# An attention and feed-forward kernel: both halves of a block's scores in one run, an older block's values behind them in the same banks

## The chip, the cores and the metric

The kernel runs on one core of one Trainium2 chip. The metric is the device time of one execution in microseconds (us); the runs of one kernel are compared by their median. Durations inside an execution come from one profiled execution, on a scale that starts at its first instruction. TensorE is called PE, VectorE DVE, ScalarE ACT, GpSimd POOL and SyncE SP, as the profile does.

## What is computed

```python
# _attn_ref: q, k, v of (8, 8, 576, 64)
scores = scale * np.matmul(q, k.transpose(0, 1, 3, 2))
mask = (rel >= 0) & (rel < window)                 # window = 128
scores = np.where(mask, scores + bias[None], -1000000000.0)   # bias: -slope of the head * |rel|
scores = scores - np.max(scores, axis=-1, keepdims=True)
attn = np.exp(scores)
attn = attn / (np.sum(attn, axis=-1, keepdims=True) + 1e-09)
return np.matmul(attn, v)
# _moe_ref: on x of (8, 576, 512), the heads side by side
mu = np.mean(x, axis=-1, keepdims=True)
var = np.mean((x - mu) ** 2, axis=-1, keepdims=True)
xn = (x - mu) / np.sqrt(var + 1e-06) * g_ln
ch = np.maximum(xn @ w_ch1, 0.0) @ w_ch2           # 512 -> 2048 -> 512
return x + ch
```

A query sees itself and the 127 keys before it.

## The kernel before

**Tiling.** Batches go in four pairs. A block is 128 queries of one batch with all 8 heads; a pair has 9 of them (`NSLOT`), the two batches in turn, and the ninth (`blk == T`) joins the last 64 queries of both. There are 36 blocks, numbered n. A block's attention is: scores of keys against queries on PE (`attend`, L495, 64x64 quarters of the array), exp on ACT (L504), the product with the table of distances on DVE (`masks`, L516), values on PE (`values_at_once`, L579: 16 matmuls, 8 for a batch's first block with its single key tile, 24 for the ninth), division by the row sum on DVE (L587, L588), centring on DVE (`centre`, L616, L620) and a transposing DMA of the result from SP (L630). `square` (L664) sums its squares on ACT.

**Scores.** An ordinary block has two key tiles, and its scores come in two halves of four heads (`attends`): each half is 16 matmuls into one `ps_sc` tile of two banks, 1024 columns in all, and one exp over all of them. `seen` gives, for a key tile, the queries that it has to be computed for: of the two halves of queries one is often left out, since the table multiplies its weights by zero. Matmuls are then 128 or 64 columns wide. The exp reads the whole tile, so columns that were left out hold older scores. A batch's first two blocks have one key tile and one score tile with all heads ("own"); the ninth block has two halves against the last two full key tiles and one more tile for its own keys ("tail", `tail_attend`). Columns of the busiest quarter of the array, for one run of 16: 384 for an ordinary half, 512 with all queries, 512 for "own", 256 for the ninth block's halves and its tail.

**Banks.** PSUM holds four banks in turn for the linear layers (`ps_mm`) and two tiles `ps_sc[0]` and `ps_sc[1]` for attention. From block 8 on, values go to `ps_sc[0]` and all scores to `ps_sc[1]`.

**Linear layers.** Blocks are gathered into groups, `GROUPS = [2] * 4 + [4] * 7`; groups 4 to 10 have four blocks, 512 columns. `mlp1(g)` makes 16 units, one for each 128 hidden channels: four matmuls (L832) into a `ps_mm` bank, then relu on ACT (L848), for units 6 and 13 on DVE (L840). `mlp2_seven(g)` makes the second layer by Strassen's seven products: 28 units of four matmuls of 256 columns (L1062), four units for each product. Products share three banks x, t and y: product 0 (units 0 to 3) starts x, and DVE drains x into the output (L1083, two instructions); product 1 (units 4 to 7) uses t; product 2 (units 8 to 11) adds onto x, on the sums of hidden blocks; product 4 (units 16 to 19) adds onto x again after a further drain. The sums of hidden blocks are DVE's (`sum_hidden`, L882), placed in `mlp1` by `SUMS_AT` behind units 5, 8, 11, 14 and 15; those of 11 need the relu of unit 10. `mlp2_last` and `mlp1_last` serve group 10.

**Order.** All engines' queues are in the order in which the code issues (`manual_schedule`). `weave_at(units, *places)` runs a linear layer unit by unit and, behind unit u, first the sums of `SUMS_AT` and then as many attention steps as u stands in `places`. Up to n = 35 each block n >= 8 has four steps: (1) loads, the masks that are still open, values of n, centring of n, the first score tile of block n + 2 with its exp; (2) the second score tile with its exp; (3) masks of the first, `square`, and `turn_natural`, which has SP transpose queries of block n + 5 and keys of n + 6 by DMA; (4) masks of the second. The places of a group's stage are

```python
    TWICE = [4, 6, 8, 9, 11, 13, 15, 15], [3, 7, 11, 15, 19, 23, 27, 27]
```

the first list for `mlp1`, the second for `mlp2_seven`: two blocks in each. In group 4 the steps of n = 12 to 16 fall, then four blocks in each group, n = 33 to 35 in group 9.

Of the kernel before, what the change touches and what calls it, by code (L numbers as in the profile page):

```python
# [13 lines left out]
AF = mybir.ActivationFunctionType  # L14
# [8 lines left out]
T = 8  # L23
# [5 lines left out]
AHEAD = 7  # L29
# [13 lines left out]


V_FIRST = 20


SUMS_AT = {
# [44 lines left out]
def kernel(  # L93
# [10 lines left out]
    nc = tc.nc  # L104
# [330 lines left out]
            dst = t[:, b] if t is q else t[:, b].rearrange("p h (c r) -> p r h c", r=2)  # L435
            copy(out=dst, in_=ps[b][:, 0 if t is q else 1])  # L436

    weights_of, unmasked, scored = {}, {}, []

    def in_halves(t):  # L440
        return t if len(t.shape) == 3 else t.rearrange("p (r c) -> p r c", r=2)

    def seen(p, blk, o, t):


        both, every = slice(0, 2), slice(0, HALF)
        first, second = slice(0, HALF // 2), slice(HALF // 2, HALF)
        if p == 0 and blk < SEEN:
            return [(0, both, every), (1, both, every)]
        if blk == T:  # L450
            batches = [slice(0, 1), slice(1, 2)]
            return [(c, batches[c if o == T else t], every) for c in range(2)]
        if o == blk:
            return [(0, both, every), (1, both, second)]
        return [(1, both, every), (0, both, first)]
# [10 lines left out]
                skip_group_check=True,  # L466
            )

    def attend(p, blk, keys, mask, tag, hps, sc=None):

        heads = slice(2 * hps[0], 2 * hps[-1] + 2)
        nk = len(keys)
        if hps[0] == 0:
            pr = probs_pool.tile([P, H, nk, P], FP16, tag=tag, name=tag)
            for t, o in enumerate(keys):
                weights_of.setdefault((p, blk), []).append((pr, t, o))  # L480
        else:
            pr = weights_of[p, blk][-1][0]
        banks = ps_sc[len(scored) % 2 if sc is None else sc]
        scored.append((p, blk))
        ps = banks.rearrange("p j (n t q) -> p j n t q", n=len(hps), t=nk)
        added = p == 0 and blk < ADDED
        qt, b = turned["q", p, blk // 2], blk % 2
        for n, hp in enumerate(hps):
            for t, o in enumerate(keys):
                kt = turned["k", p, o // 2][:, o % 2]  # L490
                for c, r, queries in seen(p, blk, o, t):
                    cols = slice(c * HALF, (c + 1) * HALF)
                    for j in range(2):
                        rows = slice(j * HALF, (j + 1) * HALF)
                        nc.tensor.matmul(  # L495
                            in_halves(ps[cols, j, n, t, :])[:, r, queries],
                            kt[rows, hp, cols],
                            in_halves(qt[rows, b, hp])[:, r, queries],
                            start=not added,
                            stop=True,  # L500
                            skip_group_check=added,
                        )
        dst = pr[:, heads].rearrange("p h t q -> p h (t q)")
        nc.scalar.activation(  # L504
            out=dst.rearrange("p (n j) q -> p j n q", j=2),
            in_=ps.rearrange("p j n t q -> p j n (t q)"),
            func=AF.Exp,
            scale=inv_sqrt_d,
        )
        if not added:  # L510
            unmasked.setdefault((p, blk), []).append((dst, mask[:, heads, :]))

    def masks(p, blk, n=3):
        todo = unmasked.get((p, blk), [])
# [17 lines left out]
    def tail_attend(p):  # L532
        return (p, T, [T], m_tail, "own", [0, 1, 2, 3])
# [4 lines left out]
    sums = {}  # L538
# [230 lines left out]
    steps += [[(scores_tail, 0)] + scores_step(9) + masks_of(8) + masks_of(9)]  # L769


    for n in range(8, count):
        ahead = place[min(n + AHEAD, count - 1)]
        todo = []
        if n + 1 < count and order[n + 1][1] == T:
            todo.append(tail_attend(order[n][0]))
        if n + 2 < count:
            todo += attends(*order[n + 2])
        step = [(load_until, ahead), (masks,) + order[n]]
        step += [(values_at_once,) + order[n]]  # L780
        if n + 3 < count and order[n + 3][1] % 2 == 0 and not by_dma(*order[n + 3]):
            step += turn_step(n + 3)
        step += [(centre,) + order[n]]
        step += [(attend, *args, 1) for args in todo[:1]]
        second = [(attend, *args, 1) for args in todo[1:]]
        third = [(masks, *args[:2], 1) for args in todo[:1]] + [(square, n)]
        for tag, m in (("q", n + 5), ("k", n + 6)):
            if m < count and order[m][1] % 2 == 0 and by_dma(*order[m]):
                p, blk = order[m]
                third.append((turn_natural, tag, p, blk // 2))  # L790
        fourth = [(masks, *args[:2], 1) for args in todo[1:]]
        if n in IN_HASTE:
            third, fourth = third[:1] + fourth, x_step(n, nc.scalar.copy) + third[1:]
        steps += [step, second, third, fourth]
    TWICE = [4, 6, 8, 9, 11, 13, 15, 15], [3, 7, 11, 15, 19, 23, 27, 27]
    LEAD = [([2, 4, 5, 6, 7, 9, 9, 10, 12, 14, 14], [3] + TWICE[1])]
    LEAD += 4 * [TWICE] + [(TWICE[0], [7, 11, 15, 19]), ([], [])]
    done = 0

    def advance_to(n):  # L800
# [52 lines left out]
    def mlp2(g, parts=((0, NFB),)):  # L853

        ht = hidden[g]
        sums = {}
        for first, end in parts:
            for at, (p, blk) in enumerate(members[g]):
                if first == 0:
                    sums[at] = ps_mm.tile([P, DM], FP32, tag="mm", name="ps_m2")  # L860
                for fb in range(first, end):
                    nc.tensor.matmul(  # L862
                        sums[at],
                        ht[:, fb, at * P : (at + 1) * P],
                        w2[:, fb, :],
                        start=(fb == 0),
                        stop=(fb == NFB - 1),
                    )
                    if fb % 2 and fb < NFB - 1:
                        yield DM  # L870
                if end == NFB:
                    finish(p, blk, sums[at])
                    yield DM
# [356 lines left out]
    def weave_at(units, *places, seven=None, sums=None, more={}):  # L1230


        advance_to(done + places.count(-1))
        for u, _ in enumerate(units):
            for f, *args in more.get(u, []):
                f(*args)
            if seven is not None:
                if u == 1:
                    inv_std(sum(GROUPS[:seven]), len(members[seven]))
                for i, c in SUMS_AT.get(u, []):  # L1240
                    sum_hidden(seven, i, c)
            if sums is not None and u % 4 == 1:
                sum_w2(sums + u // 4)
            advance_to(done + places.count(u))
# [13 lines left out]
    with tc.manual_schedule(engines={engine.PE}):  # L1258
        with tc.manual_schedule(engines={engine.Activation, engine.DVE, engine.SP, engine.Pool}):
            start()  # L1260
            advance_to(first)
            weave_at(mlp1_pair((0, 12), (0, 8), (12, NFB), (8, NFB)), 1, 2, 3, 3, 7, 7, 9, 18, 24, 28)
            weave_at(mlp2(0, ((0, 8), (8, 12), (12, NFB))), 1, 4, 8, 10, 10, 12)
            weave_at(mlp2(1), 1, 3, 5, 7, 9, 13, 13)
            weave_at(mlp1(2), 0, 4, 7, 9, 14)
            weave_at(mlp2(2), 1, 5, 9, 13, 13, 15, 15)

            weave_at(mlp1(3, (9, 10, 11)), 4, 7, 8, 10, 12, 15, sums=0)  # L1270
            weave_at(mlp2(3), 0, 2, 3, 6, 9, 11, sums=4)
            last = len(GROUPS) - 1
            for g in range(4, last):
                one, two = LEAD[g - 4]
                early, late = ({u: [(sum_w1, i)] for u, i in at.items()} for at in W1_SUMS_AT.get(g, ({}, {})))
                if g == last - 1:
                    late[20] = [(sum_x, last, i) for i in (1, 2)]
                    late[24] = [(sum_x, last, i) for i in (3, 4)]
                    late[26] = [(inv_std, sum(GROUPS[:last]), len(members[last]))]
                weave_at(mlp1(g, (6, 13)), *one, seven=g, more=early)  # L1280
                weave_at(mlp2_seven(g), *two, more=late)
            units = mlp2_last(last)
            scores_psum.close()
            ps_last = pool("ps_last", 1, space=PSUM)
            LAST_SUMS_AT = {
                u: [(sum_hidden, last, 3 + u % 2, (c, c + half // 2))]
                for u, c in ((2, 0), (4, half // 2), (3, 0), (5, half // 2))
            }
            mlp1_last(last, lambda: next(units), ps_last)
            weave_at(units, more=LAST_SUMS_AT)  # L1290
# [31 lines left out]
```

## Time and profile before

| | |
|---|---|
| runs | 309.82 us median of 3 (308.66 to 310.07) |
| profiled execution | 307.95 us |
| its span, first to last instruction | 306.2 us |
| granted PE clock | 0.993 |
| PE busy | 296.9 us (97%), 3778 matmuls |
| DVE busy | 242.8 us (79%) |
| ACT busy | 181.7 us (59%) |
| POOL busy | 112.3 us (37%) |
| chain that ended last | PE 91%, of it L832 35%, L1062 25%, L495 6%, L579 5% |

Busy time is a share of the span of that one execution. The matmuls' ends are modelled, so what a run of matmuls costs PE is read from the start of one group to the start of the next. An instruction's duration on DVE and ACT overlaps a little with the next one's; for a queue that is never idle the distance of the starts counts.

### The profile page before, as it was taken

To read this page: it belongs to the slowest core of one execution; us is meant where nothing else is said; L and a number is where in the kernel's file an instruction comes from. 1 tells how busy PE (TensorE), PEld (TensorE's weight loads), DVE (VectorE), ACT (ScalarE), POOL (GpSimd) and SP (SyncE) were. 2 spreads that over 40 slices of the span, in tenths; PEclk is the share of its full clock that TensorE was granted. 3 is DMA by queue.
4 is the path that set the end of the run, shared out by engine and by line. 5 is a ranking of instruction groups with operands and counts; after the bars stand their busy time and mean duration, and the time that the engine had idled before them with its cause. 6 is when DMAs were issued, how large, how long until landed. Compare 5 with 4: busy or idle time off the path is not lost.

```text
span 306.2 us, 9262 instructions
## 1 busy us (share of the span) xinstructions
PE 296.9 (97%) x3778; PEld 203.2 (66%) x3778; DVE 242.8 (79%) x646; ACT 181.7 (59%) x332; POOL 112.3 (37%) x153
## 2 busy tenths in 40 slices
PE   6899999999999999999999999999999999999994
PEld 2477755866755568646864686568656865698883
DVE  2588878779996799569967986798799878978983
ACT  5588776768966863675368635853586268506500
POOL 8933659763774372475107250760000000000000
PEclk9799999999999999999999999999999999999999
DMA  9999999999999999999999999999451043005014
GB/s 98 172 202 200 194 158 170 205 135 89 138 126 186 146 132 145 181 184 148 112 171 120 125 121 149 119 151 120 105 122 37 19 96 77 19 19 137 3 34 103
DMA packets 150074, 38.03 MB, mean 124 GB/s; under 512 B 140656, under 2 KB 145920, under 8 KB 150032
## 3 DMA queue, kind: packets, MB, share of 16 engines
q0 software_dynamic: 103792, 18.46, 96.0%
q1 hardware_dynamic: 45760, 18.60, 37.1%
q8 instruction: 29, 0.48, 0.7%
q10 hardware_dynamic: 480, 0.39, 0.5%
q14 instruction: 13, 0.11, 0.2%
HBM read 36.90 MB, written 9.44 MB: 151 GB/s over the span
## 4 chain that ended last, share of the span: by engine, by line
PE 91%; DMA 4%; ACT 1%; DVE 1%; POOL 1%; issue 1%; DVEq 0%; ACTq 0%; POOLq 0%
PE ps_m L832 35%; PE ps_s L1062 25%; PE ps_m L862 9%; PE ps_sc L495 6%; PE ps_sc L579 5%; PE ps_q L1141 4%; PE ps_x L956 3%; DMA q<-q 3%; DMA first<-in_k_dram 2%; PE ps_tr L343 1%; PE ps_warm L331 1%; POOL first L187 1%; PE ps_pv L550 1%; PE ps_tx L640 1%; PE ps_t L956 1%
## 5 line engine op out<-in xcount | busy, mean ns | idle before, releaser
L832 PE MATMUL ps_m<-xT,w1g 128*128 128x512 f16 (+1 forms) x512 | 103.7, 353 | 0.1
L848 ACT ACTIVATE ht_all<-ps_m 128x512 f16<-128x512 f32 (+1 forms) x143 | 71.5, 512 | 26.1 <-PE ps_m L832 24.0
L504 ACT ACTIVATE probs<-ps_sc 128x1024 f16<-128x1024 f32 x56 | 56.6, 1024 | 45.4 <-PE ps_sc L495 45.4
L832 PEld LDWEIGHTS <-w1g 128*128 128x128 f16 x512 | 47.7, 98 | 42.6 <-issue 0.3
L286 POOL DMA_DIRECT2D vx<-in_v_dram x40 | 34.1, 859 | 67.9 <-PE ps_sc L579 38.1
L1062 PE MATMUL ps_s<-w,s 128*128 128x256 f16 x384 | 43.8, 273 | 0.0
L1062 PEld LDWEIGHTS <-s 128*128 128x128 f16 x384 | 36.7, 98 | 4.7
L516 DVE TENSOR_TENSOR probs<-probs,m 128x1024 f16<-128x1024 f16 x56 | 36.9, 683 | 2.5 <-ACT probs L504 2.5
L1062 PE MATMUL ps_s<-w,ht_all 128*128 128x256 f16 x288 | 34.3, 273 | 0.0
L862 PE MATMUL ps_m<-w,ht_all 128*128 128x512 f16 x128 | 31.3, 380 | 0.0
L1062 PEld LDWEIGHTS <-ht_all 128*128 128x128 f16 x288 | 27.4, 98 | 4.9
L275 POOL DMA_DIRECT2D q<-in_q_dram x40 | 27.4, 697 | 6.0 <-DMA vx<-in_v_dram 2.2
L1083 DVE SCALAR_TENSOR_TENSOR o<-ps_s,rstd,x 128x256 f32<-128x256 f32 x48 | 21.0, 478 | 8.5 <-PE ps_s L1062 8.4
L882 DVE TENSOR_TENSOR s<-ht_all 128x1024 f16<-128x1024 f16 (+2 forms) x36 | 20.5, 571 | 7.9 <-ACT ht_all L848 6.7
L495 PE MATMUL ps_sc<-q,k 64*64 64x128 f16 (+1 forms) x1088 | 24.8, 212 | 0.6 <-ACT q L436 0.3
L495 PEld LDWEIGHTS <-k 64*64 64x64 f16 x1088 | 16.2, 108 | 13.2 <-issue 10.3
L588 DVE SCALAR_TENSOR_TENSOR x<-ps_sc,rec 128x512 f16<-128x512 f32 x32 | 22.1, 691 | 1.1
L272 POOL DMA_DIRECT2D k<-in_k_dram x20 | 17.9, 910 | 8.4 <-DMA k<-k 5.9
L664 ACT ACTIVATE junk<-xc 128x512 f16<-128x512 f16 x28 | 17.6, 628 | 5.7 <-DVE xc L620 5.6
L1083 DVE SCALAR_TENSOR_TENSOR o<-ps_s,rstd,o 128x256 f32<-128x256 f32 x36 | 15.7, 478 | 3.4 <-PE ps_s L1062 3.1
L579 PEld LDWEIGHTS <-probs 128*128 128x128 f16 x384 | 15.9, 98 | 3.6
L862 PEld LDWEIGHTS <-ht_all 128*128 128x128 f16 x128 | 11.1, 98 | 10.8
(117 smaller groups left out, 371.7 us busy)
## 6 DMA issues: line engine op xcount, KB each, us to landing
out_dram<-o SPq DMA_DIRECT2D x64, 128.0 KB, 2.5
vx<-in_v_dram POOLq DMA_DIRECT2D x32, 128.0 KB, 7.1
w<-in_moe_w_ch_dram POOLq DMA_DIRECT2D x8, 512.0 KB, 11.2
k<-in_k_dram POOLq DMA_DIRECT2D x30, 128.0 KB, 7.2
q<-in_q_dram POOLq DMA_DIRECT2D x48, 64.0 KB, 6.7
q<-in_q_dram POOLq DMA_DIRECT2D x10, 128.0 KB, 6.8
out_dram<-o SPq DMA_DIRECT2D x10, 64.0 KB, 1.9
k<-in_k_dram POOLq DMA_DIRECT2D x8, 64.0 KB, 7.7
```

Of the source, the lines that this page charges most:

```text
L275: nc.gpsimd.dma_start(out=t[half, b], in_=tokens.rearrange("h (c r) d -> r c h d", r=2)[r],)
L286: nc.gpsimd.dma_start(out=vx[p0 : p0 + n, :, 0:D], in_=v[b, :, t0 : t0 + n, :].rearrange("h p d -> p h d"),)
L495: nc.tensor.matmul(in_halves(ps[cols, j, n, t, :])[:, r, queries], kt[rows, hp, cols], in_halves(qt[rows, b, hp])[:, r, queries], start=no ...
L504: nc.scalar.activation(out=dst.rearrange("p (n j) q -> p j n q", j=2), in_=ps.rearrange("p j n t q -> p j n (t q)"), func=AF.Exp, scale=in ...
L516: nc.vector.tensor_tensor(out=dst, in0=dst, in1=mask, op=ALU.mult)
L579: nc.tensor.matmul(ps[:, h, 0 : D + 1], pr[:, h, t, :], vext[(p * NSLOT + o) % NV][:, h, :], start=(n == 0), stop=(n == len(terms) - 1),)
L588: nc.vector.scalar_tensor_tensor(out=x.rearrange("p (h d) -> p h d", h=H), in0=ps[:, :, 0:D], scalar=1.0, in1=rec.unsqueeze(2).broadcast_t ...
L832: nc.tensor.matmul(ps[:, 0:cols], w[:, kb, fb * P : (fb + 1) * P], xT[:, kb, 0:cols], start=(kb == 0), stop=(kb == NKB - 1),)
L848: nc.scalar.activation(out=ht[:, fb, :], in_=ps[:, 0:cols], func=AF.Relu)
L862: nc.tensor.matmul(sums[at], ht[:, fb, at * P : (at + 1) * P], w2[:, fb, :], start=(fb == 0), stop=(fb == NFB - 1),)
L1062: nc.tensor.matmul(ps[:, pair, :], lhs[:, fb, at : at + P], rhs[:, fb, :], start=(first and pair == 0 and fb == 0), stop=(fb == half - 1), ...
L1083: nc.vector.scalar_tensor_tensor(out=outs[at][:, cols], in0=ps[:, pair], scalar=rstd[:, n : n + 1], in1=(xs[p, blk] if fresh else outs[at] ...
```

## The change

From n = 12 (`ONE_GO`) on, a block's four steps are cut anew. (1) Both score tiles of block n + 2 in one run: the first goes to `ps_sc[1]` with all its queries (`full`), its exp is issued at once; the second goes to `ps_sc[0]` with the queries that are seen, and its exp is put off. (2) `exps`: the put-off exp. (3) Loads, open masks, values of n, now into `ps_sc[1]`, and centring. (4) Masks of both tiles, `square`, `turn_natural` (for n = 12 this last one goes with step 3). Where block n has one score tile only, it goes to `ps_sc[0]` and its exp is put off. For n = 12 both tiles have all their queries. The places change with it: two steps of n = 12 go into `mlp2(3)`, and the steps of a stage's block lie behind units 1, 2, 4, 7 and 8, 9, 11, 13 of `mlp1`, and 0, 2, 5, 8 and 12, 14, 19, 23 of `mlp2_seven`.

```diff
+ONE_GO = 12
...
-    weights_of, unmasked, scored = {}, {}, []
+    weights_of, unmasked, scored, scored_only = {}, {}, [], []
...
-    def seen(p, blk, o, t):
+    def seen(p, blk, o, t, all_of_it):
...
-        if p == 0 and blk < SEEN:
+        if all_of_it or p == 0 and blk < SEEN:
             return [(0, both, every), (1, both, every)]
...
-    def attend(p, blk, keys, mask, tag, hps, sc=None):
+    def attend(p, blk, keys, mask, tag, hps, sc=None, full=False, put_off=False):
...
-                for c, r, queries in seen(p, blk, o, t):
+                for c, r, queries in seen(p, blk, o, t, full):
...
-        nc.scalar.activation(
-            out=dst.rearrange("p (n j) q -> p j n q", j=2),
-            in_=ps.rearrange("p j n t q -> p j n (t q)"),
-            func=AF.Exp,
-            scale=inv_sqrt_d,
-        )
+
+        def weights():
+            nc.scalar.activation(
+                out=dst.rearrange("p (n j) q -> p j n q", j=2),
+                in_=ps.rearrange("p j n t q -> p j n (t q)"),
+                func=AF.Exp,
+                scale=inv_sqrt_d,
+            )
+
+        if put_off:
+            scored_only.append(weights)
+        else:
+            weights()
...
+    def exps():
+
+        while scored_only:
+            scored_only.pop()()
...
-    for n in range(8, count):
+    for n in range(8, ONE_GO):
...
+    for n in range(ONE_GO, count):
+        todo = []
+        if n + 1 < count and order[n + 1][1] == T:
+            todo.append(tail_attend(order[n][0]))
+        if n + 2 < count:
+            todo += attends(*order[n + 2])
+        first_of, pairs = n == ONE_GO, (1, 0) if len(todo) > 1 else (0,)
+        go = [(attend, *a, sc, first_of or sc == 1, sc == 0) for a, sc in zip(todo, pairs)]
+        step = [(load_until, place[min(n + AHEAD, count - 1)]), (masks,) + order[n]]
+        step += [(values_at_once, *order[n], 1), (centre,) + order[n]]
+        rest = [(masks, *args[:2], 1) for args in todo] + [(square, n)]
+        for tag, m in (("q", n + 5), ("k", n + 6)):
+            if m < count and order[m][1] % 2 == 0:
+                p, blk = order[m]
+                (step if first_of else rest).append((turn_natural, tag, p, blk // 2))
+        steps += [go, [(exps,)], step, rest]
+    TWICE = [1, 2, 4, 7, 8, 9, 11, 13], [0, 2, 5, 8, 12, 14, 19, 23]
+    LEAD = [([2, 4, 4, 5, 7, 9, 9, 10, 12, 14], TWICE[1])]
+    LEAD += 4 * [TWICE] + [(TWICE[0], TWICE[1][:4]), ([], [])]
...
-            weave_at(mlp2(3), 0, 2, 3, 6, 9, 11, sums=4)
+            weave_at(mlp2(3), 0, 2, 3, 6, 9, 11, 12, 14, sums=4)
```

More of the change, by code (lines that the diff above doesn't have):

```diff
@@ L794 @@
         steps += [step, second, third, fourth]
-    TWICE = [4, 6, 8, 9, 11, 13, 15, 15], [3, 7, 11, 15, 19, 23, 27, 27]
-    LEAD = [([2, 4, 5, 6, 7, 9, 9, 10, 12, 14, 14], [3] + TWICE[1])]
-    LEAD += 4 * [TWICE] + [(TWICE[0], [7, 11, 15, 19]), ([], [])]
+    for n in range(ONE_GO, count):
[17 more added lines that the diff above has]
+    LEAD += 4 * [TWICE] + [(TWICE[0], TWICE[1][:4]), ([], [])]
     done = 0
```

## The prediction

> **What bounds the kernel now.** I read the page first: who is busy, and whether TensorE is held back.
>
> ```profile
> PE 296.9 (97%) x3778; PEld 203.2 (66%) x3778; DVE 242.8 (79%) x646; ACT 181.7 (59%) x332; POOL 112.3 (37%) x153
> ...
> PEclk9799999999999999999999999999999999999999
> ```
>
> TensorE (PE) is the bound, at full clock. Then the windows, cut at the starts of `mlp1` of groups 4 to 10, where the change acts:
>
> ```profile
> 155.39:186.53 31.14, 31.14 (x371) 20.89 (x369) 24.83 (x64) 18.55 (x30) 12.48 (x16) 1.00 1.43 136
> ```
>
> All six are like this one, of group 6: PE never idle, no wait of PE anywhere. So time can be won only by fewer or denser PE instructions, and lost by any wait that gets through. Third, the timeline of PE in that stage:
>
> ```profile
> 162.72 4.49 PE L832 MATMUL ps_m<-xT,w1g 128*128 128x512 f16 x20
> 167.05 0.65 PE L579 MATMUL ps_sc<-vx,probs 128*128 128x65 f16 x16
> 167.63 0.37 PE L495 MATMUL ps_sc<-q,k 64*64 64x128 f16 x16
> 167.93 1.90 PE L832 MATMUL ps_m<-xT,w1g 128*128 128x512 f16 x8
> 169.76 0.37 PE L495 MATMUL ps_sc<-q,k 64*64 64x128 f16 x16
> 170.06 1.90 PE L832 MATMUL ps_m<-xT,w1g 128*128 128x512 f16 x8
> 171.80 1.91 PE L1062 MATMUL ps_s<-w,ht_all 128*128 128x256 f16 x16
> ...
> 176.58 1.59 PE L1062 MATMUL ps_s<-w,s 128*128 128x256 f16 x13
> ```
>
> Read the starts. Sixteen score matmuls hold PE 0.30 (167.63 to 167.93). Eight L832 before scores take 1.83 (167.93 to 169.76), before more matmuls of full size 1.74 (170.06 to 171.80): entering a score run costs 0.09 more. Sixteen value matmuls take 0.58 before scores and so 0.49 by themselves. A whole run elsewhere:
>
> ```profile
> 37.55 0.64 PE L495 MATMUL ps_sc<-q,k 64*64 64x128 f16 x32
> 38.12 0.82 PE L862 MATMUL ps_m<-w,ht_all 128*128 128x512 f16 x3
> ```
>
> Both halves, all queries, in one go: 0.57. Last, VectorE (DVE) and ScalarE (ACT) in group 6:
>
> ```profile
> 167.01 0.56 DVE L882 TENSOR_TENSOR s<-ht_all 128x768 f16<-128x768 f16 x1 [0.70 <-ACT ht_all L848]
> ...
> 173.55 0.43 DVE L882 TENSOR_TENSOR s<-ht_all,s 128x512 f16<-128x512 f16 x1
> 173.89 1.29 DVE L516 TENSOR_TENSOR probs<-probs,m 128x1024 f16<-128x1024 f16 x2
> 175.10 0.87 DVE L1083 SCALAR_TENSOR_TENSOR o<-ps_s,rstd,x 128x256 f32<-128x256 f32 x2
> ```
> ```profile
> 165.15 0.62 ACT L664 ACTIVATE junk<-xc 128x512 f16<-128x512 f16 x1
> 165.67 0.19 ACT L664 ACTIVATION_READ_ACCUMULATOR junk<-xc 128x1 f32 x1
> 165.76 1.22 ACT L848 ACTIVATE ht_all<-ps_m 128x512 f16<-128x512 f32 x2
> 167.25 0.60 ACT L848 ACTIVATE ht_all<-ps_m 128x512 f16<-128x512 f32 x1 [0.27 <-PE ps_m L832]
> 168.06 1.02 ACT L504 ACTIVATE probs<-ps_sc 128x1024 f16<-128x1024 f32 x1 [0.21 <-PE ps_sc L495]
> ```
>
> This is the hidden second path. The hidden-layer sums of unit 11 (L882) start at 167.01, when the relu of unit 10 ends (the second of the two at 165.76). From there DVE has no pause until the first output drain (L1083) ends at 175.97, 8.96 later. That drain empties the bank onto which the s-product (L1062 `w,s`, unit 8 of `mlp2_seven`) then adds at 176.58. Slack: 0.61. Likewise in groups 4, 5, 7, 8, 9: 0.21, 0.23, 0.89, 0.61, 0.30. Nothing shows it, since nobody waits yet.
>
> **The change, part by part.** *Scores, on PE.* An ordinary block pays 2 x (0.30 + 0.09) = 0.79 now. After: one entry, 0.09, and one run of 32, the first half with all queries, the second with those seen. The run's cost lies between rows: 0.57 (all queries, 37.55) and 0.47 (69.06, tail and own together). A run goes with the columns of its busiest quarter of the array: 1024 and 768 there, 512 + 384 = 896 here, so 0.52. Saved: 0.79 - 0.61 = 0.18. From n = 12 to 33 there are 14 such blocks: 2.5. Block 12 has all queries in both halves: 0.13. Three blocks whose todo is a batch's last, short block: narrow runs of 0.25 (182.41 to 182.67) become one of 512 + 256 = 768 columns, 0.47: 0.69 - 0.56, 0.13 each. Two with tail and own: 0.25 + 0.34 + 0.19 against 0.57 + 0.09: 0.12 each. Single ones: nothing. Sum 2.5 + 0.13 + 0.39 + 0.24 = 3.3 us gained. Bounds: only the entries saved, 20 x 0.09 = 1.8; 0.47 for every run, 4.2. I take 3.3, as columns explain the rows on both sides.
>
> *Values.* Same matmuls, now without scores behind them. They go to bank 1, behind the first half's exp, and the next scores there wait until DVE has read the values; behind either wait stands the whole linear stream. Counted as below, the exp is done at least 0.3 ahead (values at unit 5 of `mlp2_seven`; 0.9 or more elsewhere) and the reading at least 0.7. Free; were the 0.3 gone, PE would wait there what it then doesn't wait at unit 8.
>
> *Exps, on ACT.* Each takes ACT 0.94 (start to next start, 168.06 to 169.00). Same number, but moved: in `mlp1` from behind units 4, 6, 11, 13 to 1, 2, 8, 9. That puts two between the relus of units 8 and 10. Counted from the end of unit 7, with 0.20 from a unit's end to its relu, 0.51 from a relu to the next instruction (0.60 to its own end), 0.61 for the square (165.15 to 165.76): relu 7 at 0.20, square 0.71, relu 8 at 1.32, exp 1.83, relu 9 at 2.77, exp 3.28, relu 10 at 4.22, done 4.82. Its sums start at 4.85. Before: the x20 from 162.72 to 167.05 are units 7 to 11, 0.866 each, so unit 7 ended at 163.58 and the sums started 3.43 after. The two exps cost this path 1.42.
>
> *Masks, on DVE.* Two of 0.60 go ahead of the sums of 14 and 15 instead of behind; both places are ahead of the drain, so its 8.96 stay.
>
> *The meeting point.* After: 4.85 + 8.96 = 13.81 from unit 7's end until the bank is free, and 0.05 until PE knows (in the chain of waits `xc` ends at 13.68 and L640 starts at 13.73). PE gets there after 8 x 0.863 + 0.61 + 0.49 (rest of `mlp1`) and 0.61 + 0.49 + 8 x 0.437 (`mlp2_seven`) = 12.6. **PE waits 1.26.** The saving itself brings PE there earlier. The same count for the others, as start of the sums + DVE's length - PE's way: group 4, 5.1 + 8.9 - 13.0, 1.1 (other places); group 5, 4.9 + 8.9 - 12.1, 1.7 (block 18 has 8 value matmuls, not 16); group 7, 4.5 + 8.3 - 12.4, 0.4 (a single score tile: one exp and one mask less); group 8 as 6, 1.3; group 9, 4.4 + 8.3 - 12.0, 0.8 (likewise, and PE has no scores in `mlp2_seven`). In sum 6.6. Made for the kernel before, it gives slacks of 0.28, 0.13, 0.58, 0.87, 0.58, 0.20, within 0.1 of the trace's. The late DVE is met again at unit 16: from the first drain's end, values, centre and drain (2.23), two masks, now ahead of the third drain (1.2), and that drain (0.87) make 4.3, PE's way is 8 x 0.437 + 0.61 = 4.1. So 0.2 in groups 4 to 8, 1.0 (the windows show group 9 with fewer DVE instructions there). Loss 7.6. Bounds: 0, if relu 10 weren't delayed; 10, with 0.4 more in each of six groups.
>
> *The rest.* `turn_natural` (SP), loads (POOL), `square` move by a few units. Closest: n = 13's scores, some 3 us earlier, at 97.8, on queries whose transposes are issued at 85.96 and 88.07; landing takes 6.7 in the median, 9.8 at most: by 97.9 at worst, 0.1 once. In steady state queries are turned 15 us ahead. DVE, ACT, SP work beside block 12's first steps in `mlp2(3)` is covered by PE.
>
> *Sum.* 7.6 - 3.3 = 4.3; the trace's six slacks together are 0.2 above the count's, so 4.1 more. The profiled execution, 307.95 (span 306.2, 1.75 around it), becomes 312.05. It lies 1.87 under the median of the runs, 309.82, which becomes **313.9**.
>
> ACT empties all score banks; in a group of 31 us its 18.6 busy are no bound, only units 8 to 10 are. The Trainium skill (TensorEngine Tiling (Array Packing), section PSUM Bottleneck) warns that packing the array speeds TensorE but not the emptying of PSUM, and advises to share that between ScalarE and VectorE; taken as an average it costs nothing here and would leave the gain of 3.3, taken locally it is the delay above.
>
> **Rivals.** *Faster: the drain isn't late.* Place: unit 8 of `mlp2_seven`; price: none of the 7.6 is paid, 309.8 - 3.3 = 306.5. It decides at sums starting 12.6 - 9.0 = 3.6 after unit 7; I have 4.85, so ACT would have to be over an exp earlier. For it: slack today everywhere. Against: queue order is program order in every row above. 0.10.
>
> *About the same: PE waits only for the first of the drain's two instructions.* The trace has one wait, at the product's first matmul, and can't tell for which. Then each of the six waits is 0.39 shorter and the five of 0.2 are gone: 313.9 - 2.3 - 1.0 = 310.6. 0.12.
>
> *Slower still: the run of 32 saves only its entries.* A second half that follows with other widths may run as it does alone, 0.30 and 0.35 back to back: gain 1.8, not 3.3, at 315.4. For it: no row has such a mix. Against: both rows of 32 are well under twice a run of 16. 0.10.
>
> **Numbers.** A measurement here can tell about 0.5%, 1.55 us. Forecast 0.68, its own range 312.3 to 315.4 (0.25 each way in the six waits). 8 in 10: from 310.0, which leaves out the faster rival and a third of the second, to 315.8, which leaves out part of the last. Faster 0.10; within 0.5% 0.12; slower 0.78.
>
> **What would show it.** Right: L1062 `w,s` with some 7 us idle before it, released by DVE's drain; in ACT two exps with one relu between them, ahead of relu 10; score runs of 32 at 0.52; PE's busy time some 3 us less. Wrong: no idle of PE there (then the span is near 303), or PE waiting at scores or values instead.

## The result, and the profile after

The changed kernel takes 310.23 us in the median of 22 runs, the kernel before 308.64 in as many: ratio 1.0054, 95% interval 1.0034 to 1.0075. It is slower, as forecast, by some 1.7 us instead of 4.1; the forecast of 1.3% is outside the interval. The page's first line and the waits of PE between 88 and 303:

```profile
PE 294.2 (96%) x3778; PEld 201.2 (65%) x3778; DVE 240.2 (78%) x646; ACT 177.3 (58%) x332; POOL 112.7 (37%) x153
```
```profile
PE ps_s L1096 <- DVE o L1117: 3.6, 5, 1.3
```

PE is busy 2.7 less (296.9 before) and now waits, at one line alone: the s-products (L1096, was L1062) for DVE's drain (L1117, was L1083). The timeline of PE in group 6:

```profile
165.22 0.59 PE L498 MATMUL ps_sc<-q,k 64*64 64x128 f16 x32
165.75 2.76 PE L866 MATMUL ps_m<-xT,w1g 128*128 128x512 f16 x12
168.35 0.65 PE L594 MATMUL ps_sc<-vx,probs 128*128 128x65 f16 x16
...
176.02 1.04 PE L1096 MATMUL ps_s<-w,ht_all 128*128 128x256 f16 x8
177.72 2.34 PE L1096 MATMUL ps_s<-w,s 128*128 128x256 f16 x20 [0.65 <-DVE o L1117]
```

Both halves now hold PE 0.52 in one run (0.523, from 165.22 to 165.75). Eight matmuls from 176.02 take 0.87, so PE could have gone on at 176.89 or 176.90; it does at 177.72, 0.82 later. (The bracket says 0.65, because a matmul's modelled end lies beyond the next one's start; for the same reason the list above has five waits and 3.6 us, and leaves out the shortest. I count waits by starts.) ACT and DVE ahead of it:

```profile
164.47 0.60 ACT L882 ACTIVATE ht_all<-ps_m 128x512 f16<-128x512 f32 x1 [1.13 <-PE ps_m L866]
164.96 0.62 ACT L679 ACTIVATE junk<-xc 128x512 f16<-128x512 f16 x1
165.48 0.19 ACT L679 ACTIVATION_READ_ACCUMULATOR junk<-xc 128x1 f32 x1
165.57 0.59 ACT L882 ACTIVATE ht_all<-ps_m 128x512 f16<-128x512 f32 x1
166.05 1.02 ACT L509 ACTIVATE probs<-ps_sc 128x1024 f16<-128x1024 f32 x1
166.95 0.61 ACT L882 ACTIVATE ht_all<-ps_m 128x512 f16<-128x512 f32 x1
167.43 1.04 ACT L509 ACTIVATE probs<-ps_sc 128x1024 f16<-128x1024 f32 x1
168.33 1.11 ACT L882 ACTIVATE ht_all<-ps_m 128x512 f16<-128x512 f32 x2
```
```profile
168.99 0.56 DVE L916 TENSOR_TENSOR s<-ht_all 128x768 f16<-128x768 f16 x1 [2.52 <-ACT ht_all L882]
...
172.08 0.68 DVE L874 TENSOR_SCALAR ht_all<-ps_m 128x512 f16<-128x512 f32 x1
172.68 1.28 DVE L531 TENSOR_TENSOR probs<-probs,m 128x1024 f16<-128x1024 f16 x2
173.88 0.55 DVE L916 TENSOR_TENSOR s<-ht_all 128x768 f16<-128x768 f16 x1
...
176.79 0.87 DVE L1117 SCALAR_TENSOR_TENSOR o<-ps_s,rstd,x 128x256 f32<-128x256 f32 x2
```

Relu 7 (the relu of unit 7, at 164.47), square, relu 8, exp, relu 9, exp, relu 10 (the first of the two at 168.33): the queue of the prediction. DVE idles 2.52 for relu 10, then works to the drain's end at 177.66 without waiting for another engine, and PE follows 0.06 later. These 8.67 from the start of the sums to the drain's end are called DVE's stretch below.

For a comparison that the first 90 us don't blur, I take the stretch from the turn of block 11 in `mlp2(3)` (L640, L655) to the first matmul of group 10 (L956, L990). It is 186.88 before (90.35 to 277.23) and 188.38 after (90.08 to 278.46), 1.50 more. The waits at unit 8 in groups 4 to 9 are 0.89, 1.44, 0.82, 0.05, 0.82, 0.46, in sum 4.48; at unit 16 in groups 4 to 8 0.03, 0.08, 0.13, 0.08, 0.08, in sum 0.40. Without them the stretch is 183.50: the scores gained 3.38.

### The profile page after: what moved, and what is told of

It reads as the page before. It is cut to its first block, busy times and chain, and to the rows that moved or that the text cites. A ratio compares the mean times of both kernels' runs of the same rounds, so it can differ in the third digit from the quotient of the medians.

```text
span 307.4 us, 9278 instructions
## 1 busy us (share of the span) xinstructions
PE 294.2 (96%) x3778; PEld 201.2 (65%) x3778; DVE 240.2 (78%) x646; ACT 177.3 (58%) x332; POOL 112.7 (37%) x153
## 4 chain that ended last, share of the span: by engine, by line
PE 71%; DVE 13%; ACT 6%; DMA 3%; POOL 3%; issue 3%; DVEq 0%; POOLq 0%
PE ps_m L866 26%; PE ps_s L1096 19%; PE ps_m L896 9%; DVE s L916 7%; PE ps_sc L498 4%; PE ps_q L1175 4%; DMA w<-in_moe_w_ch_dram 3%; PE ps_sc L594 3%; PE ps_x L990 3%; ACT probs L509 2%; ACT ht_all L882 2%; DVE o L1117 1%; DVE x L603 1%; DVE probs L531 1%; DVE ht_all L874 1%
## 5 line engine op out<-in xcount | busy, mean ns | idle before, releaser
L882 ACT ACTIVATE ht_all<-ps_m 128x512 f16<-128x512 f32 (+1 forms) x143 | 70.3, 514 | 31.0 <-PE ps_m L866 29.0
L509 ACT ACTIVATE probs<-ps_sc 128x1024 f16<-128x1024 f32 x56 | 55.6, 1025 | 8.6 <-PE ps_sc L498 8.6
L1096 PE MATMUL ps_s<-w,s 128*128 128x256 f16 x384 | 45.0, 273 | 3.6 <-DVE o L1117 3.6
L1096 PEld LDWEIGHTS <-s 128*128 128x128 f16 x384 | 36.8, 98 | 9.4 <-issue 4.5
L531 DVE TENSOR_TENSOR probs<-probs,m 128x1024 f16<-128x1024 f16 x56 | 36.2, 683 | 2.0 <-ACT probs L509 2.0
L1096 PE MATMUL ps_s<-w,ht_all 128*128 128x256 f16 x288 | 35.3, 273 | 0.0
L1096 PEld LDWEIGHTS <-ht_all 128*128 128x128 f16 x288 | 27.4, 98 | 4.6
L498 PE MATMUL ps_sc<-q,k 64*64 64x128 f16 (+1 forms) x1088 | 21.7, 212 | 0.8 <-DVE k L420 0.3
L1117 DVE SCALAR_TENSOR_TENSOR o<-ps_s,rstd,x 128x256 f32<-128x256 f32 x48 | 20.9, 476 | 1.6 <-PE ps_s L1096 1.5
L1117 DVE SCALAR_TENSOR_TENSOR o<-ps_s,rstd,o 128x256 f32<-128x256 f32 x36 | 15.7, 478 | 5.7 <-PE ps_s L1096 5.6
L602 DVE RECIPROCAL rec<-ps_sc 128x8 f32<-128x8 f32 x32 | 6.5, 202 | 16.5 <-PE ps_sc L594 16.4
```

Of the source, the lines that this page charges most:

```text
L498: nc.tensor.matmul(in_halves(ps[cols, j, n, t, :])[:, r, queries], kt[rows, hp, cols], in_halves(qt[rows, b, hp])[:, r, queries], start=no ...
L509: nc.scalar.activation(out=dst.rearrange("p (n j) q -> p j n q", j=2), in_=ps.rearrange("p j n t q -> p j n (t q)"), func=AF.Exp, scale=in ...
L531: nc.vector.tensor_tensor(out=dst, in0=dst, in1=mask, op=ALU.mult)
L882: nc.scalar.activation(out=ht[:, fb, :], in_=ps[:, 0:cols], func=AF.Relu)
L1096: nc.tensor.matmul(ps[:, pair, :], lhs[:, fb, at : at + P], rhs[:, fb, :], start=(first and pair == 0 and fb == 0), stop=(fb == half - 1), ...
L1117: nc.vector.scalar_tensor_tensor(out=outs[at][:, cols], in0=ps[:, pair], scalar=rstd[:, n : n + 1], in1=(xs[p, blk] if fresh else outs[at] ...
```

## The experiments

Stretches and waits, all from the starts of matmuls, with the ratio to the kernel before:

| kernel | ratio, 95% interval | stretch | waits at unit 8 | at unit 16 | other | stretch less waits |
|---|---|---|---|---|---|---|
| before | 1 | 186.88 | 0 | 0 | | 186.88 |
| changed | 1.0054 (1.0034 to 1.0075) | 188.38 | 4.48 | 0.40 | | 183.50 |
| e1 | 0.9979 (0.9957 to 1.0001) | 185.61 | 1.81 | 0.33 | | 183.47 |
| e2 | 1.0131 (1.0099 to 1.0164) | 190.99 | 4.82 | 0.61 | 2.06 | 183.50 |
| e3 | 0.9922 (0.9891 to 0.9953) | 183.71 | 0.11 | 0.11 | | 183.49 |
| e4 | 1.0067 (1.0043 to 1.0092) | 188.82 | 5.02 | 0.32 | | 183.48 |
| e5 | 0.9960 (0.9931 to 0.9989) | 185.03 | 1.23 | 0.33 | | 183.47 |
| e6 | 1.0027 (0.9999 to 1.0055) | 188.32 | 0.68 | 0.11 | 0.67 | 186.86 |
| e7 | 1.0028 (1.0005 to 1.0050) | 188.10 | 0 | 0 | | 188.10 |
| e8 | a single run | 188.01 | 4.52 | 0 | | 183.49 |

**e1: one exp less ahead of relu 10.**

```diff
-    TWICE = [1, 2, 4, 7, 8, 9, 11, 13], [0, 2, 5, 8, 12, 14, 19, 23]
-    LEAD = [([2, 4, 4, 5, 7, 9, 9, 10, 12, 14], TWICE[1])]
+    TWICE = [1, 2, 4, 7, 8, 11, 11, 13], [0, 2, 5, 8, 12, 14, 19, 23]
+    LEAD = [([2, 4, 4, 5, 7, 9, 9, 11, 12, 14], TWICE[1])]
```

> The changed kernel with the put-off exp of mlp1's second block behind unit 11 instead of 9 (in group 4 behind 11 instead of 10), so that one exp less stands ahead of the relu of unit 10. Theory A (ACT's queue order delays the sums of unit 11, DVE passes the delay on to the first drain): the sums start some 0.9 us earlier after unit 7's end (3.8 instead of 4.7), PE's waits at unit 8 of the second layer go from 0.90, 1.44, 0.82, 0.05, 0.82, 0.45 in groups 4 to 9 to 0, 0.5, 0, 0, 0, 0; 3.9 us less than the changed kernel, about 306.3, so about 0.75% faster than the kernel before. Rival B (the new place of the masks or DVE's length alone makes the drain late): the waits stay, 310.2.

The waits were 0.89, 0.59, 0.13, 0, 0.14, 0.06. Theory A holds, rival B falls: an exp's place on ACT decides over PE's waits at the other end of DVE's queue. Two sizes were off. The sums start 4.04 after unit 7 in groups 5, 6 and 8, not 3.8: relu 10 now waits for its own unit (three units of 0.863 and the score run of 0.52 + 0.09 are 3.2, then 0.2, then 0.6). And group 4 didn't move at all: behind unit 10 the exp already stood behind relu 10, so my edit there changed nothing on this path. The stretch is 2.77 shorter than the changed kernel's instead of the 3.9 expected, and the time, 0.2% under the kernel before instead of 0.75%, isn't clearly faster: the interval just reaches 1.

**e2: the masks behind the sums again.**

```diff
-    TWICE = [1, 2, 4, 7, 8, 9, 11, 13], [0, 2, 5, 8, 12, 14, 19, 23]
+    TWICE = [1, 2, 4, 7, 8, 9, 11, 15], [0, 2, 5, 8, 12, 14, 19, 23]
```

> The changed kernel with the last step of mlp1's second block (masks, square, turn) behind unit 15 instead of 13, so that the masks stand behind the sums of 14 and 15 again, as before the change. Theory A1 (DVE's stretch from the sums to the drain was shorter than in the kernel before, 8.67 instead of 8.96, since a mask now stands between the relu of unit 13 and the sums that read it, and covers a pause between the two): the stretch is 8.95 again, the waits at unit 8 grow by 0.27 in groups 5, 6 and 8 and by 0.1 to 0.3 in 7 and 9; some 1.1 us slower than the changed kernel, 311.3. Rival: the length is the sum of the operations, whatever their order; 310.2, waits unchanged.

DVE in group 6 of this kernel:

```profile
174.23 0.68 DVE L874 TENSOR_SCALAR ht_all<-ps_m 128x512 f16<-128x512 f32 x1
175.02 0.56 DVE L916 TENSOR_TENSOR s<-ht_all 128x768 f16<-128x768 f16 x1
```

From the relu of unit 13 to the next start it takes 0.79, since the sums read what the relu writes; in the changed kernel, with a mask next, 0.60 (172.08 to 172.68). The kernel before has the same 0.79:

```profile
170.10 0.68 DVE L840 TENSOR_SCALAR ht_all<-ps_m 128x512 f16<-128x512 f32 x1
170.89 0.56 DVE L882 TENSOR_TENSOR s<-ht_all 128x768 f16<-128x768 f16 x1
...
172.07 0.56 DVE L882 TENSOR_TENSOR s<-ht_all,s 128x768 f16<-128x768 f16 x1
172.63 0.43 DVE L882 TENSOR_TENSOR s<-ht_all 128x512 f16<-128x512 f16 x1
```
```profile
172.00 0.60 ACT L848 ACTIVATE ht_all<-ps_m 128x512 f16<-128x512 f32 x1 [0.27 <-PE ps_m L832]
```

DVE's stretch is 8.86 and 8.87 in groups 6 and 8 instead of 8.67, and the waits grow by 0.20, 0.19, 0.21, 0.19 in groups 5 to 8. So A1 holds for 0.2 of the 0.29. The other 0.1 is a second pause, which A1 didn't name: in the kernel before the sums of 15 start 0.56 after the instruction ahead of them (172.07 to 172.63), just behind the end of the relu of unit 15 on ACT (172.60), which they read. In the changed kernel (175.06 to 175.54) and in e2 it is 0.48, since DVE gets there later, when that relu has long ended. The two pauses make 0.19 + 0.08 = 0.27.

In group 9 something not expected came: there the values of n = 35 wait 1.42 for the mask of their "own" weights, which stood too far back, and unit 8 then waits for nothing. A DMA of `xT` cost 0.64 more. These two make 2.06 of the 2.61 by which the stretch is longer than the changed kernel's, where 1.1 was expected.

**e3: e1, and the relu of unit 13 on ACT.**

```diff
-                weave_at(mlp1(g, (6, 13)), *one, seven=g, more=early)
+                weave_at(mlp1(g, (6,)), *one, seven=g, more=early)
```

> As e1_exp_behind_11, and the relu of unit 13 in groups 4 to 9 on ACT instead of DVE. Theory A: 0.6 us less in DVE's stretch from the sums of 11 to the drain, so no wait at unit 8 in any group, and none at unit 16; 4.9 us less than the changed kernel, about 305.3, so about 1.1% faster than the kernel before: the whole gain of the denser score runs shows. Rival C (ACT becomes the bound when it takes another relu; the sums of 14 wait for it): waits at unit 8 of 0.5 and more, 306.5 to 308.

DVE's stretch is 8.07 in groups 4, 5, 6 and 8; PE's only listed wait between 86 and 303 is another one:

```profile
PE ps_sc L498 <- DMA q<-q: 0.5, 1, 0.5
```

It lies before the stretch (at 87.88). Rival C falls. The stretch is 3.17 shorter than before the change, nearly the whole gain, and the kernel is 0.8% faster than the kernel before, where 1.1% was expected, at the edge of its interval. It beats both kernels.

**e4: the second exp not put off.**

```diff
-        go = [(attend, *a, sc, first_of or sc == 1, sc == 0) for a, sc in zip(todo, pairs)]
+        go = [(attend, *a, sc, first_of or sc == 1, False) for a, sc in zip(todo, pairs)]
```

> The changed kernel with the second half's exp issued right behind its scores, not put off: both exps now stand ahead of the relu of unit 9, still both ahead of that of unit 10. Theory A: the relu of unit 10 ends at the same time, waits at unit 8 as in the changed kernel (4.5 in sum), 310.2 within 0.3. Rival D (what costs is that a relu between is late and a bank of the first layer comes free late): the relu of unit 9 is 0.9 later, PE waits in mlp1 and the time rises by 1 us or more.

Groups 6 and 8 are as in the changed kernel, 0.81 and 0.82, with sums at 4.72 in both; nothing waits in `mlp1`, so rival D falls. Group 4 waits 2.06 instead of 0.89: here the exp goes from behind relu 10 to ahead of it, and the sums start at 5.97 instead of 5.05, one exp later. That is e1's lesson from the other side. DVE's stretch there is 0.24 longer too (9.11 instead of 8.87), and in group 5 it is 0.16 shorter and the wait 1.28 instead of 1.44; the cause of that stays open. Groups 7 and 9, with single score tiles, have their exp earlier and wait less (0, 0.05).

**e5: the relu of unit 13 alone.** On the changed kernel, with its own places:

```diff
-                weave_at(mlp1(g, (6, 13)), *one, seven=g, more=early)
+                weave_at(mlp1(g, (6,)), *one, seven=g, more=early)
```

> The changed kernel with only the relu of unit 13 moved from DVE to ACT in groups 4 to 9; the exps stay behind units 9 and 10. Theory A (a wait at unit 8 is start of the sums + DVE's stretch - PE's way): the start stays 4.7 after unit 7's end, the stretch falls from 8.67 to 8.07, so the waits of 0.89, 1.44, 0.82, 0.05, 0.82, 0.46 become about 0.1, 0.7, 0.2, 0, 0.2, 0; 3.3 us less than the changed kernel. Rival B (only the order of the exps matters): waits as in the changed kernel.

The waits were 0.11, 0.68, 0.22, 0, 0.22, 0, the start of the sums stayed at 4.72, DVE's stretch was 8.07, and the kernel's stretch fell by 3.35. A wait here is start + DVE's stretch - PE's way. The two cures act on different terms, and e3 has both: 4.04 and 8.07.

**e6: the slack of the kernel before.**

```diff
-                weave_at(mlp1(g, (6, 13)), *one, seven=g, more=early)
+                weave_at(mlp1(g, (6, 12, 13)), *one, seven=g, more=early)
```

> The kernel before with one more relu on DVE (unit 12 in groups 4 to 9, from ACT), 0.6 us in the stretch between the sums of 11 and the first drain. Theory A (the slack read from the trace of before is real and is all there is): 0.21, 0.24, 0.61, 0.89, 0.62, 0.30 minus 0.6 minus 0.05 gives waits at unit 8 of 0.44, 0.41, 0.04, 0, 0.03, 0.35, 1.3 us in sum; ratio to the kernel before 1.004. Rival G (PE waits for less than the whole drain, so there is more cover than that): no wait, ratio 1.000.

Waits at unit 8: 0.18, 0.40, 0, 0, 0, 0.10. In group 9 a further 0.25 stands just ahead of it: the values of n = 35 (L579, at 268.11) wait for the mask of their "own" weights, the last instruction ahead of the drain in DVE's queue (L516, ends at 268.04). Groups 6 and 8 keep 0.10 and 0.11 of slack, as 0.5 more DVE work against 0.61 says; group 4 lost less than thought, because its stretch grew by 0.34 only. Rival G falls: the cover read from the trace was all there was. The starts decide this, not the ratio, whose interval holds both 1.000 and 1.004. (A DMA of `xT` cost 0.42.)

**e7: the width alone.** In the kernel before, `seen` and `attend` take a flag as in the change, and

```diff
-        step += [(attend, *args, 1) for args in todo[:1]]
+        step += [(attend, *args, 1, n >= 12 and len(todo) > 1) for args in todo[:1]]
```

> The kernel before with only the width of the change: from n = 12 the first of two score tiles has all its queries; two runs, old banks, old places. Theory A (a run goes with the columns of the busiest quarter): 0.30 becomes 0.35 in 15 blocks and 0.25 becomes 0.35 in 5, so 1.25 us more on PE, ratio 1.004. Rival H (a run goes with its number of matmuls, the width is free): 0, ratio 1.000, and the gain of the change would be a matter of the entries and run lengths alone.

The timeline of PE:

```profile
102.10 0.42 PE L495 MATMUL ps_sc<-q,k 64*64 64x128 f16 x16
102.45 1.90 PE L832 MATMUL ps_m<-xT,w1g 128*128 128x512 f16 x8
104.28 0.37 PE L495 MATMUL ps_sc<-q,k 64*64 64x128 f16 x16
104.58 0.60 PE L832 MATMUL ps_m<-xT,w1g 128*128 128x512 f16 x2
```

All queries 0.35, those seen 0.30. The stretch grew by 1.22 (1.25 expected). Width costs; rival H falls.

**e8: the masks behind the third drain.**

```diff
-    TWICE = [1, 2, 4, 7, 8, 9, 11, 13], [0, 2, 5, 8, 12, 14, 19, 23]
+    TWICE = [1, 2, 4, 7, 8, 9, 11, 13], [0, 2, 5, 12, 12, 14, 19, 23]
```

> The changed kernel with the masks of the second layer's first block (with square and turn) behind unit 12 of mlp2_seven instead of 8, so that they stand behind the third drain. One look at the trace, not for the time. Theory A: the waits at unit 16, 0.03, 0.08, 0.13, 0.08, 0.08 in groups 4 to 8, vanish, since 1.2 us of masks no longer stand between the second drain and the third; the waits at unit 8 stay (0.89, 1.44, 0.82, 0.05, 0.82, 0.46); from the first matmuls of n = 12's stage to group 10, 0.4 us less. Rival: the third drain is late because of the first one's lateness alone; the waits at unit 16 stay.

The waits at unit 16 are gone, those at unit 8 stay (4.52), the stretch is 0.37 shorter: theory A.

## Why the prediction was right or wrong

*The gain, right.* 3.3 forecast, 3.38 measured; the run of 32 costs 0.52, as the columns of the busiest quarter say. The rival of the entries alone falls with it, and e7 shows the width's price by itself.

*The mechanism, right.* Two exps ahead of relu 10, sums late, first drain late, PE waits at unit 8, and lightly at unit 16. e1, e4 and e5 move each link. Of the rivals, "faster" fails since the sums started at 4.7, not under 3.6; "only the first of the drain's two instructions" fails too: PE went on at 177.72, just behind the second (177.66), not behind the first (176.79 + 0.48).

*The sizes of the waits, wrong: 7.6 forecast, 4.9 measured, so 4.1 net instead of 1.5.* Unlike the gain, the loss is a small difference of long queues (13.8 against 12.6), and a few per cent of a queue more than doubled the net.

- Start of the sums: 4.85 forecast, 4.72 measured. Fully packed, ACT takes 0.48 from a relu (165.57 to 166.05) and 0.90 from an exp (166.05 to 166.95), not the 0.51 and 0.94 that I took from rows of a queue with gaps. Over six groups 0.6.
- DVE's stretch: "both places are ahead of the drain, so its 8.96 stay" was the wrong step, and the largest error. It is 8.67 in groups 6 and 8: the old order had two pauses within it, 0.19 behind the relu of unit 13, where a mask now stands, and 0.08 for the relu of unit 15. Over six groups 1.2. e2 brings the first pause back in groups 6 and 8.
- The rest of unit 8, 0.3, is spread over PE's way, about 0.05 later per group than counted.
- Unit 16: 1.0 forecast, 0.40 measured. The mechanism was as said (e8), the size again a difference of 4.3 and 4.1.
- The base: the sum started from 309.82, the median of three runs; that of 22 is 308.64. Of the 3.7 between 313.9 and 310.23 this is 1.2, and nearly all the rest is the waits. Laid out from 308.64, the forecast's own range would be 311.1 to 314.2 and still be missed.

*Covers that held.* The values' wait for the first exp, the scores' wait for the reading of the values, and the queries of n = 13 never held PE in the changed kernel.

## What to carry to other kernels

Here PE was never idle, and the edit's gain could be read from rows to a few per cent (3.3 against 3.38); what an edit costs on the queues behind has to be laid out as start + queue - arrival, and its error is that of the queues, not of their difference: give the range accordingly. Ask of each moved instruction which dependent work stands behind it in its own queue, and what that work releases several instructions later. When the wait is found, shorten either queue: an exp behind the relu that others wait for took 2.77 off here (e1), one relu on the engine with room 3.35 (e5), and both together brought nearly the whole gain out (e3).

## What the runs showed of the hardware

The same DVE relu of 128 x 512 takes 0.60 to the next start when the next instruction doesn't read its output, and 0.79 when it does. The Trainium skill (VectorE: DVE Perf Modes, section The DRAIN you can't avoid) says that the pipe is emptied behind every instruction, though a next one that isn't held starts earlier, and that in a chain of copies semaphores between them cost nothing extra. Here the dependent pair was 0.19 dearer, in the kernel before and in e2 alike, and an independent mask between the two covered it. The measurement decides.

The first 90 us differ by up to 3.8 between profiled executions of these kernels (the turn of block 11 begins between 89.30 in e6 and 93.13 in e5), more than the changed kernel's 1.50 or the gain's 3.38. A stretch that begins behind them, less its waits, agrees within 0.03 in all kernels with the change's scores (183.47 to 183.50), and within 0.02 in the kernel before and e6.
